# Attention with decay and a feed-forward block: plain float32 scores for eight heads, and another pace for the weights

## The chip, the cores and the metric

The kernel runs on one NeuronCore of a Trainium2 chip. TensorE (PE) multiplies matrices and transposes through an identity, VectorE (DVE), ScalarE (ACT) and GpSimd (POOL) do the elementwise work, and SyncE (SP) issues all DMA transfers of this kernel, in program order. Each engine runs its own instructions in order and waits on semaphores for the others. The metric is the device time of one execution, in microseconds (us).

## The reference

There are 8 batches of 8 heads, 576 tokens, 64 numbers a head. With `q`, `k`, `v` and a forget gate `f`:

```python
scores = scale * np.matmul(q, k.transpose(0, 1, 3, 2))      # scale = 1/8
log_f = np.log(np.clip(f, 0.0001, 1.0))
cum = np.cumsum(log_f, axis=-1)
decay = cum[:, :, :, None] - cum[:, :, None, :]
scores = np.where(causal, -1000000000.0, scores + decay)
scores = scores - np.max(scores, axis=-1, keepdims=True)
attn = np.exp(scores)
attn = attn / (np.sum(attn, axis=-1, keepdims=True) + 1e-09)
out = np.matmul(attn, v)
```

The heads of a batch are put side by side as `x` (4608 tokens of 512), and a block with a hidden layer of 2048 follows:

```python
xn = (x - mean) / np.sqrt(var + 1e-06) * g_ln
return x + np.maximum(xn @ w_ch1, 0.0) @ w_ch2
```

All is float32, except that the two weight matrices come as float64. `q` and `k` are some six times larger than in a usual draw, about 0.6 in spread.

## The kernel before, in words

**Precision.** Two ways of multiplying are used. In one, an operand is split into a high part (type `fp32r`, made by a copy on ScalarE) and the remainder (a subtraction on GpSimd or VectorE), and products of the parts are added up in PSUM. In the other, plain float32 operands go straight into the matmul. The heads 0 to 15 (`h.full`, `NFULL = 16`) use plain float32 for attention times v (`av_unit`, L464); the heads 16 to 63 use split operands there (L486). The scores use split operands in all heads.

**Preparing a head's scores.** `load` (L303) brings `raw`, both q and k transposed, with the 64 rows present twice on the 128 partitions. `prep_a` copies k to its high part (L323) and loads two decay rows into `kl` (L322, for head 0 L119); `prep_b` subtracts for k's remainder on GpSimd (L326) and copies q (L330); `prep_c` moves q's high part by DMA into `xq` (L333) and subtracts for q's remainder on GpSimd (L334). There is one `raw` buffer, and there are two each of `hi`, `kl` and `xq`. `xq` has two rows of ones at its end (L319), which meet the decay rows. A score tile is then two matmuls (L353 of 128 rows, L354 of 66 rows) over the same columns; a head has 64 + 192 + 320 + 448 + 576 = 1600 columns in five tiles.

**Slots.** A head is four slots, t = 1 to 4; slot u = 4n + t - 1. Slot t = 1 computes two query tiles (64 and 128 queries), the others one of 128. In a slot, a string of letters (`ORDERS`) gives the order in which the pieces are issued, the same order on every engine. Until slot 37 it is `WwQsSthAeMrgFBmlLNPaRf`. Q is the score matmuls; S the masked minimum of the negative scores on VectorE (L377); e the exponential on ScalarE (L388); B the reciprocal of the row sum on VectorE (L393, L394) and the scaling on GpSimd (L395). t transposes the tile of two slots ago on PE (L401), h copies the transposes on ScalarE (L451), A is attention times v of three slots ago. P prepares later heads: `prep_a`, `prep_b`, `prep_c` of the next head in t = 1, 2, 3, and the raw load of the head after it in t = 4. M, r, m, N, R are the feed-forward part ("MoE steps").

**Weights.** The float64 weights come as pairs of 32-bit words and are turned to float32 on the chip, in 32 items (16 of each matrix, taking turns). One item is started in each tick of `WPrep.tick`. An item costs one scaling on ScalarE (L162), three integer operations on VectorE (L172, L173, L176), a copy to its high part on ScalarE (L213) and a remainder on GpSimd (L217); items of the first matrix also have eight matmul records for column sums (L188) and four operations on VectorE (L196). The letter W calls ticks until a due count is reached:

```python
due = 1 + min(u, W_CHANGE) / W_SLOTS + max(0, u - W_CHANGE) * W_TICKS
while not wp.done() and wp.tick_no <= due:
    wp.tick()
```

Its operations are put in a queue, from which w, g and f take one, two and three in each slot; a new tick first empties the queue. All ticks together are 38.

**MoE steps.** A chunk is 256 tokens; there are 18 chunks of 16 steps. A step is 12 matmuls into the hidden layer (L563 to L565), a relu and its remainder (L571 on ScalarE, L576 on VectorE), and six matmuls of the step before (L585 to L587). At most one step is made in each slot from slot 35 on (`FIRST_MOE`), if its data are there: step j of a chunk needs 2(j + 1) weight items, where `ready()` counts the ticks less five. Chunks 0 and 1 need batch 0 alone, the next ones later batches. What is left when the slots are over follows in a loop of its own.

Of the kernel before, what the change touches and what calls it, by code (L numbers as in the profile page):

```python
# [8 lines left out]
F32 = mybir.dt.float32  # L9
F32R = mybir.dt.float32r  # L10
# [5 lines left out]
B, H, S, D = 8, 8, 576, 64  # L16
# [7 lines left out]
S1 = 320  # L24
NEG = -1.0e9
SCALE = 1.0 / 8.0
NFULL = 16
W2_LOW = 3
W2_WAIT = 2
# [2 lines left out]
FIRST_MOE = 35  # L32
WARM = 36

W_SLOTS, W_CHANGE, W_TICKS = 1.85, 68, 1.1
W_RAW, W_FLOAT = 3, 5
W_BORROW = 2
W_SUMS = 2
# [19 lines left out]
def attn_moe(ctx: ExitStack, tc: tile.TileContext, qk, v, f, g, w1, w2, out):  # L58
    nc = tc.nc

    const = ctx.enter_context(tc.tile_pool(name="const", bufs=1))
    work = ctx.enter_context(tc.tile_pool(name="work", bufs=1))
# [6 lines left out]
    mm = nc.tensor.matmul  # L69

    def bank(name):
        return ps.tile([P, 512], F32, tag="b", bufs=6, name=name)
# [12 lines left out]
    for i in range(WARM):  # L85
# [4 lines left out]
        out=mask[:, S - P :], in_=mask[:, S - P :], pattern=[[-1, P]], base=0,  # L90
# [9 lines left out]
    cumr = work.tile([B * H, 2, S], F32R, tag="ph2", bufs=1, name="cumr")  # L100
    cumd = dram.tile([B * H, 2, S], F32, tag="cumd", name="cumd")
# [9 lines left out]
    def gates(h0):  # L111
        nc.vector.tensor_scalar(out=fa, in0=fa, scalar1=1e-4, scalar2=1.0, op0=ALU.max, op1=ALU.min)
        nc.scalar.activation(fb, fa, AF.Ln)
        nc.vector.tensor_tensor_scan(out=fc, data0=fones, data1=fb, initial=0.0, op0=ALU.mult, op1=ALU.add)
        nc.scalar.activation(cumr[:, 0, :], fc, AF.Copy, scale=-1.0 / SCALE)
        nc.vector.scalar_tensor_tensor(
            out=cumr[:, 1, :], in0=fc, scalar=-1.0 / SCALE, in1=cumr[:, 0, :].bitcast(F32), op0=ALU.mult, op1=ALU.subtract
        )
        nc.sync.dma_start(out=h0.kl[64:66, :].bitcast(F32), in_=cumr[0:1].bitcast(F32))  # L119
        nc.sync.dma_start(out=cumd, in_=cumr.bitcast(F32))  # L120


# [2 lines left out]
    def consts():  # L125
        nc.sync.dma_start(out=gcol, in_=g)
        nc.gpsimd.memset(gneg, -1.0 / DM)
        nc.gpsimd.tensor_tensor(
            out=gneg.rearrange("p (k c) -> p k c", k=KT), in0=gneg.rearrange("p (k c) -> p k c", k=KT),
            in1=gcol.rearrange("p (k o) -> p k o", o=1).broadcast_to((P, KT, P)), op=ALU.mult,  # L130
        )
# [162 lines left out]
    class Head:  # L294
        pass

    xqs = []

    def load(n):
        h = Head()  # L300
        h.n, h.full = n, n < NFULL
        h.raw = late.tile([P, 2, S], F32, tag="raw", bufs=1, name=f"raw{n}")
        nc.sync.dma_start(out=h.raw, in_=qk[n])  # L303
        return h
# [8 lines left out]
    def prep_a(h):  # L313
        n = h.n
        h.hi = late.tile([P, 2, S], F32R, tag="hi", bufs=2, name=f"hi{n}")
        h.kl = work.tile([66, S], F32R, tag="kl", bufs=2, name=f"kl{n}")
        if len(xqs) < 2:
            xqs.append(work.tile([66, S], F32R, tag="xq", bufs=2, name=f"xq{n}"))
            nc.gpsimd.memset(xqs[n][64:66, :].bitcast(F32), 1.0)  # L319
        h.xq = xqs[n % 2]  # L320
        if n > 0:
            nc.sync.dma_start(out=h.kl[64:66, :].bitcast(F32), in_=cumd[n])  # L322
        nc.scalar.copy(out=h.hi[:, 1, :], in_=h.raw[:, 1, :])  # L323

    def prep_b(h):
        nc.gpsimd.tensor_tensor(  # L326
            out=h.kl[0:64, :], in0=h.raw[0:64, 1, :], in1=h.hi[0:64, 1, :].bitcast(F32), op=ALU.subtract
        )

        nc.scalar.copy(out=h.hi[:, 0, :], in_=h.raw[:, 0, :])  # L330

    def prep_c(h):
        nc.sync.dma_start(out=h.xq[0:64, :].bitcast(F32), in_=h.hi[0:64, 0, :].bitcast(F32))  # L333
        nc.gpsimd.tensor_tensor(  # L334
            out=h.hi[64:128, 0, :], in0=h.raw[64:128, 0, :], in1=h.hi[64:128, 0, :].bitcast(F32), op=ALU.subtract
        )
# [8 lines left out]
    def qk_mm(h, t):  # L345
        q0, m, w = QT[t]
        cuts = [(0, w)] if w <= 512 else [(0, w // 2), (w // 2, w)]
        h.s = getattr(h, "s", {})
        h.s[t] = []
        for i, (a, z) in enumerate(cuts):  # L350
            sp = bank(f"s{h.n}_{t}_{i}")[:m, : z - a]
            xq, kl = h.xq[:, q0 : q0 + m], h.kl[:, a:z]
            mm(sp, h.hi[:, 0, q0 : q0 + m], h.hi[:, 1, a:z], start=True, stop=False)  # L353
            mm(sp, xq, kl, start=False, stop=True)  # L354
            h.s[t].append((a, z, sp))

    corners = []
# [9 lines left out]
    def softmax_a(h, t):  # L367
# [8 lines left out]
        for i, (a, z, sp) in enumerate(h.s[t]):  # L376
            nc.vector.tensor_tensor_reduce(  # L377
                out=pt[:m, a:z], in0=sp, in1=mask[:m, off + a : off + z], scale=-SCALE,
                scalar=3.0e38 if i == 0 else st[:m, 0:1], op0=ALU.add, op1=ALU.min, accum_out=st[:m, i : i + 1],
# [69 lines left out]
    def transposed_hi(h, t):  # L449
        for tp, hi, lo in h.parts:  # L450
            nc.scalar.copy(out=hi, in_=tp)  # L451
# [280 lines left out]
    hd = {}  # L732

    def start_head(n):
        hd[n] = load(n)
# [4 lines left out]
    wp.load(1)  # L740
    load_v(hd[0])
    consts()
    prep_a(hd[0])
    prep_b(hd[0])
    prep_c(hd[0])
    start_head(1)
    gates(hd[0])
    wp.tick()
    for u, slot in enumerate(slots):

        def before(k):
            return slots[u - k] if u >= k else None

        if slot is not None:
            n, t = slot
            h = hd[n]
        av = None
        if before(LAG + 1) is not None and before(LAG + 1)[1] in (2, 4):
            av = hd[before(LAG + 1)[0]]
        moe.fetch_low(ALL if wp.done() else wp.ready())  # L760
        want = moe.can(wp.ready()) and u >= FIRST_MOE

        def piece(c):
            tu = before(LAG)
            if c == "t" and tu is not None:
                transpose_unit(hd[tu[0]], tu[1])
            elif c == "h" and tu is not None:
                transposed_hi(hd[tu[0]], tu[1])
            elif c == "l" and tu is not None:
                transposed_lo(hd[tu[0]])  # L770
            elif c == "Q" and slot is not None:
                if t == 1:
                    qk_mm(h, 0)
                qk_mm(h, t)
            elif c == "A" and av is not None:
                av_unit(av, before(LAG + 1)[1])
            elif c == "S" and slot is not None:
                if t == 1:
                    softmax_a(h, 0)
                softmax_a(h, t)  # L780
            elif c == "e" and slot is not None:
                if t == 1:
                    softmax_e(h, 0)
                softmax_e(h, t)
            elif c in FILL:
                wp.fill(FILL[c])
            elif c == "s":
                wp.sums()
            elif c == "F" and av is not None:
                finish(av)  # L790
            elif c == "a" and av is not None:
                finish_add(av)
            elif c == "r" and want:
                moe.first_high()
            elif c == "R":
                moe.limit = min(NCHUNK, max(0, u - LAG - 1) // (4 * H) * S // C)
                moe.rest()
            elif c == "L":
                run_later(RSTD)
            elif c == "M" and want:  # L800
                moe.first()
            elif c == "B" and slot is not None:
                if t == 1:
                    softmax_b(h, 0)
                softmax_b(h, t)
            elif c == "m" and want:
                moe.first_low()
            elif c == "W":
# [3 lines that stand above are left out]
            elif c == "N":  # L812
                moe.second()
            elif c == "P":
                prep()

        def prep():

            if slot is not None:
                if n + 1 < B * H:  # L820
                    if t == 1:
                        prep_a(hd[n + 1])
                    if t == 2:
                        prep_b(hd[n + 1])
                    if t == 3:
                        prep_c(hd[n + 1])
                if t == 4 and n + 2 < B * H:
                    start_head(n + 2)
                if not h.full and t == LAG + 1:
                    prep_v(h)  # L830
                if t == LAG + 1 and n + 1 < B * H:
                    load_v(hd[n + 1])

        for c in [o for first, o in ORDERS if first <= u][-1]:
            piece(c)
# [48 lines left out]
```

## Time and profile before

| | |
|---|---|
| median of 3 runs | 1301.36 us (1301.26 to 1301.51) |
| profiled execution | 1305.8 us |
| its span, first to last instruction | 1304.0 us |
| PE / DVE / ACT / POOL busy, share of the span | 95% / 61% / 50% / 35% |
| mean granted clock of TensorE | 0.962 |
| DMA moved | 194.33 MB, 149 GB/s |

Busy time counts how long an engine has an instruction in it. For PE the ends of matmuls are modelled, since they are pipelined: the distance between two starts says more than a duration. "PEclk" or "granted clock" is the share of the full clock that TensorE got. A row of an instruction group reads: line, engine, operation, output <- inputs, shape and count, then busy time and mean duration in ns, then the idle time of the engine just before and what ended it. A row of the timeline reads: start, duration, engine, line, operation, and in brackets the idle time before it with its releaser. "SPq" rows are the issue of a DMA by SyncE.

### The profile page before, as it was taken

The page shows a single profiled execution, that of the slowest core. Times are in us where ns is not written, and L with a number is a line of the kernel's source. Part 1 is how long each engine was busy: PE and PEld are TensorE (multiplying, and loading weights), DVE is VectorE, ACT ScalarE, POOL GpSimd, SP SyncE. Part 2 cuts the span into 40 slices and gives each one's busy share as a digit, 9 for nine tenths or more (in the row PEclk, how much of TensorE's full clock was granted, in tenths as well). Part 3 has the DMA queues.
Part 4 walks back from the last instruction along what each step waited for, and adds up shares of the span by engine and source line. Part 5 has one row for each costly group of instructions (what it writes and reads, how often), then busy time and mean ns, then how long its engine had stood idle before and what let it go on. Part 6 is the DMA issues. An engine that isn't in the chain of part 4 may idle for free.

```text
span 1304.0 us, 25602 instructions
## 1 busy us (share of the span) xinstructions
PE 1243.2 (95%) x8148; PEld 1099.5 (84%) x8148; DVE 794.0 (61%) x2868; ACT 657.8 (50%) x1937; POOL 450.5 (35%) x543
## 2 busy tenths in 40 slices
PE   4888698989999999999999999999999999999998
PEld 4565486669999999998999999999999999999997
DVE  4776757756767676767676767676767652232232
ACT  4666556655555555655555555555556531111111
POOL 4556545544343434343334343434343400000000
PEclk7777799999999999999999999999999999999999
DMA  4565466335454545454545454544554434444433
GB/s 151 159 207 174 148 208 178 111 127 162 137 172 135 175 134 175 134 175 134 175 134 175 133 175 134 169 140 156 152 158 151 152 103 141 122 124 127 131 117 94
DMA packets 139895, 194.33 MB, mean 149 GB/s; under 512 B 32496, under 2 KB 81648, under 8 KB 139760
## 3 DMA queue, kind: packets, MB, share of 16 engines
q1 hardware_dynamic: 139760, 192.69, 47.8%
q8 instruction: 65, 1.06, 0.3%
q14 instruction: 70, 0.57, 0.1%
HBM read 159.82 MB, written 23.36 MB: 140 GB/s over the span
## 4 chain that ended last, share of the span: by engine, by line
PE 79%; DVE 6%; DMA 6%; ACT 4%; POOL 2%; issue 2%; SPq 0%; POOLq 0%; ACTq 0%; DVEq 0%
PE h L564 10%; PE h L563 10%; PE acc L585 9%; PE h L565 9%; PE acc L586 9%; PE acc L587 9%; PE tr L401 6%; PE o L486 5%; DMA raw<-in_qk_dram 4%; PE s L353 3%; PE o L464 3%; PE s L354 3%; ACT p L388 1%; POOL hi L334 1%; PE xp L401 1%
## 5 line engine op out<-in xcount | busy, mean ns | idle before, releaser
L395 POOL TENSOR_SCALAR p<-p,st 64x64 f32<-64x64 f32 (+4 forms) x320 | 176.2, 553 | 566.6 <-DVE st L394 266.1
L563 PE MATMUL h<-x,w1h 128*128 128x256 f32 x1152 | 329.9, 286 | 4.4 <-ACT x L547 4.4
L564 PE MATMUL h<-x,w1h 128*128 128x256 f32 x1152 | 327.0, 284 | 1.2 <-DVE x L548 0.6
L565 PE MATMUL h<-x,w1l 128*128 128x256 f32 x1152 | 325.2, 282 | 0.0
L571 ACT ACTIVATE hh<-h 128x256 fp32r<-128x256 f32 x288 | 110.7, 384 | 311.4 <-PE h L565 307.5
L576 DVE SCALAR_TENSOR_TENSOR hh<-h,hh 128x256 fp32r<-128x256 f32 x288 | 121.6, 422 | 212.4 <-ACT hh L571 204.5
L585 PE MATMUL acc<-w2h,hh 128*128 128x512 f32 x576 | 229.2, 398 | 0.6 <-ACT hh L571 0.6
L563 PEld LDWEIGHTS h<-x,w1h 128*128 128x128 f32 x1152 | 218.4, 190 | 10.7 <-ACT x L547 5.4
L586 PE MATMUL acc<-w2s,hh 128*128 128x512 f32 x576 | 227.3, 395 | 0.0
L587 PE MATMUL acc<-w2h,hh 128*128 128x512 f32 x576 | 226.6, 393 | 0.0
L564 PEld LDWEIGHTS h<-x,w1h 128*128 128x128 f32 x1152 | 218.7, 190 | 6.6 <-DVE x L548 3.0
L565 PEld LDWEIGHTS h<-x,w1l 128*128 128x128 f32 x1152 | 218.5, 190 | 0.0
L388 ACT ACTIVATE p<-p,st 64x64 f32<-64x64 f32 (+4 forms) x320 | 178.4, 559 | 62.2 <-DVE st L377 59.1
L451 ACT CAST ph<-tr 64x128 fp32r<-64x128 f32 (+4 forms) x384 | 108.9, 333 | 119.3 <-PE tr L401 88.9
L353 PE MATMUL s<-hi 128*128 128x288 f32 (+4 forms) x384 | 132.7, 366 | 37.8 <-POOL hi L334 35.4
L401 PE MATMUL tr<-identr,p 128*128 128x128 f32 (+1 forms) x896 | 147.4, 283 | 4.0 <-POOL p L395 3.2
L377 DVE CUSTOM_DVE_ANT_0 p<-s,mask 64x64 f32<-64x64 f32 (+4 forms) x320 | 130.6, 420 | 14.6 <-PE s L354 13.1
L587 PEld LDWEIGHTS acc<-w2h,hh 128*128 128x128 f32 x576 | 108.7, 189 | 25.6 <-DVE st L393 0.2
L401 PEld LDWEIGHTS tr<-identr,p 128*128 128x128 f32 (+1 forms) x896 | 105.5, 135 | 24.7 <-POOL p L395 5.4
L456 DVE TENSOR_TENSOR ph<-tr,ph 64x192 fp32r<-64x192 f32 x192 | 57.8, 301 | 106.5 <-ACT ph L451 104.1
L585 PEld LDWEIGHTS acc<-w2h,hh 128*128 128x128 f32 x576 | 109.3, 190 | 14.2 <-issue 0.8
L586 PEld LDWEIGHTS acc<-w2s,hh 128*128 128x128 f32 x576 | 109.5, 190 | 12.4
(79 smaller groups left out, 1900.3 us busy)
## 6 DMA issues: line engine op xcount, KB each, us to landing
w2s<-w2d SPq DMA_DIRECT2D x288, 256.0 KB
raw<-in_qk_dram SPq DMA_DIRECT2D x64, 576.0 KB
wr<-in_w_dram SPq DMA_DIRECT2D x32, 512.0 KB
vr<-in_v_dram SPq DMA_DIRECT2D x64, 160.0 KB
xq<-hi SPq DMA_DIRECT2D x64, 144.0 KB
out_dram<-xt SPq DMA_DIRECT2D x36, 256.0 KB
xa<-xs SPq DMA_DIRECT2D x32, 160.0 KB
w2d<-wl SPq DMA_DIRECT2D x16, 256.0 KB
```

Source lines behind the costliest of these rows:

```text
L353: mm(sp, h.hi[:, 0, q0 : q0 + m], h.hi[:, 1, a:z], start=True, stop=False)
L377: nc.vector.tensor_tensor_reduce(out=pt[:m, a:z], in0=sp, in1=mask[:m, off + a : off + z], scale=-SCALE, scalar=3.0e38 if i == 0 else st[: ...
L388: nc.scalar.activation(pt[:m, :w], pt[:m, :w], AF.Exp, bias=st[:m, i : i + 1], scale=-1.0, accum_out=st[:m, 2:3])
L395: nc.gpsimd.tensor_scalar(out=pt[:m, :w], in0=pt[:m, :w], scalar1=st[:m, 3:4], scalar2=1.0, op0=ALU.mult, op1=ALU.mult)
L401: nc.tensor.transpose(out_, in_, ident[:m, :m])
L563: mm(ph, w1h[:, k, fs], c.x[k][:, 0, :], start=(k == 0), stop=False)
L564: mm(ph, w1h[:, k, fs], c.x[k][:, 1, :], start=False, stop=False)
L565: mm(ph, w1l[:, k, fs], c.x[k][:, 0, :], start=False, stop=(k == KT - 1))
L576: nc.vector.scalar_tensor_tensor(out=h[:, 1, :], in0=ph, scalar=0.0, in1=h[:, 0, :].bitcast(F32), op0=ALU.max, op1=ALU.subtract)
L585: mm(c.acc[i], h[:, 0, ts_], w2h[:, j, :], start=(j == 0), stop=False)
L586: mm(c.acc[i], h[:, 0, ts_], low, start=False, stop=False)
L587: mm(c.acc[i], h[:, 1, ts_], w2h[:, j, :], start=False, stop=(j == FT - 1))
```

## The change

For the heads 0 to 7 (`NPLAIN = 8`) q and k are loaded straight into `xq` and `kl` as float32, 64 rows each, together with the decay rows, by three DMAs issued in slot t = 1 of the head before. There is no `raw`, no high part and no remainder for these heads, and a score tile is one plain float32 matmul of 66 rows in place of two. The heads from 8 on are prepared as before. At the start, the preparation of head 0 and the load of head 1's `raw` ahead of the gate computation go away. The weights' due count is changed to 1 + u / 2.4 until slot 34, and from there on 0.95 ticks are added in each slot; before, it was 1 + u / 1.85 until slot 68.

```diff
+NPLAIN = 8
...
-W_SLOTS, W_CHANGE, W_TICKS = 1.85, 68, 1.1
+W_SLOTS, W_CHANGE, W_TICKS = 2.4, 34, 0.95
...
-    xqs = []
+    xqs, xfs = [], []
+
+    def new_xq(name, dt):
+        xq = work.tile([66, S], dt, tag="xq", bufs=2, name=name)
+        nc.gpsimd.memset(xq[64:66, :].bitcast(F32), 1.0)
+        return xq
 
     def load(n):
         h = Head()
-        h.n, h.full = n, n < NFULL
+        h.n, h.plain, h.full = n, n < NPLAIN, n < NFULL
+        if h.plain:
+            h.kl = work.tile([66, S], F32, tag="kl", bufs=2, name=f"kl{n}")
+            if len(xfs) < 2:
+                xfs.append(new_xq(f"xf{n}", F32))
+            h.xq = xfs[n % 2]
+            nc.sync.dma_start(out=h.xq[0:64, :], in_=qk[n][0:64, 0, :])
+            nc.sync.dma_start(out=h.kl[0:64, :], in_=qk[n][0:64, 1, :])
+            if n > 0:
+                nc.sync.dma_start(out=h.kl[64:66, :], in_=cumd[n])
+            return h
...
-            mm(sp, h.hi[:, 0, q0 : q0 + m], h.hi[:, 1, a:z], start=True, stop=False)
-            mm(sp, xq, kl, start=False, stop=True)
+            if h.plain:
+                mm(sp, xq, kl, start=True, stop=True)
+            else:
+                mm(sp, h.hi[:, 0, q0 : q0 + m], h.hi[:, 1, a:z], start=True, stop=False)
+                mm(sp, xq, kl, start=False, stop=True)
...
     consts()
-    prep_a(hd[0])
-    prep_b(hd[0])
-    prep_c(hd[0])
-    start_head(1)
     gates(hd[0])
...
-                if n + 1 < B * H:
+                if t == 1 and n + 1 < NPLAIN:
+                    start_head(n + 1)
+                if NPLAIN <= n + 1 < B * H:
                     if t == 1:
                         prep_a(hd[n + 1])
...
-                if t == 4 and n + 2 < B * H:
+                if t == 4 and NPLAIN <= n + 2 < B * H:
                     start_head(n + 2)
```

More of the change, by code (lines that the diff above doesn't have):

```diff
@@ L118, in gates @@
         )
-        nc.sync.dma_start(out=h0.kl[64:66, :].bitcast(F32), in_=cumr[0:1].bitcast(F32))
+        nc.sync.dma_start(out=h0.kl[64:66, :], in_=cumr[0:1].bitcast(F32))
         nc.sync.dma_start(out=cumd, in_=cumr.bitcast(F32))
@@ L317, in prep_a @@
         if len(xqs) < 2:
[L318 to L322, printed above, removed]
+            xqs.append(new_xq(f"xq{n}", F32R))
+        h.xq = xqs[(n - NPLAIN) % 2]
+        nc.sync.dma_start(out=h.kl[64:66, :].bitcast(F32), in_=cumd[n])
         nc.scalar.copy(out=h.hi[:, 1, :], in_=h.raw[:, 1, :])
```

## The prediction

> **What bounds the kernel now.** I read the clock by slices first, then the span cut at the starts of heads 0, 1, 8 and 18, then the waits of the first stretch, then single instructions.
>
> ```profile
> PEclk7777799999999999999999999999999999999999
> ```
> ```profile
> 134.55 0.31 PE L353 MATMUL s<-hi 128*64 128x64 f32 x1 [3.61 <-POOL hi L334]
> ...
> 300.19 0.28 PE L353 MATMUL s<-hi 128*64 128x64 f32 x1
> ```
> ```profile
> 0.00:19.40 19.40, 7.24 (x38) 6.87 (x38) 7.58 (x8) 7.58 (x9) 7.50 (x15) 0.79 0.47 149
> 19.40:31.60 12.20, 6.01 (x26) 5.22 (x26) 7.80 (x28) 6.63 (x19) 5.23 (x7) 0.64 0.54 164
> 31.60:134.60 103.00, 83.26 (x358) 57.75 (x358) 73.72 (x230) 66.23 (x191) 62.23 (x64) 0.73 0.56 173
> 134.60:300.20 165.60, 148.07 (x846) 114.27 (x846) 109.61 (x360) 98.25 (x291) 84.96 (x91) 0.92 0.52 160
> 300.20:1304.00 1003.80, 998.65 (x6887) 915.40 (x6884) 595.24 (x2244) 479.12 (x1430) 290.63 (x367) 1.00 0.47 145
> ```
> The columns are the stretch, its length, busy time of PE, PEld, DVE, ACT and POOL, the granted clock, DMA share and GB/s. The 64-query score matmul opens each head, so the two rows above date heads 8 and 18. From 300.2 us on PE is busy for 998.65 of 1003.80 us at full clock: whatever matmul work is left there sets the end, and each MoE step done earlier comes straight off it. The loss lies ahead: at 134.6 us no MoE step has run, and PE was idle for a fifth of the time and slow for much of the rest.
>
> ```profile
> PE s L353 <- POOL hi L334: 24.4, 8, 4.7
> ...
> DVE st L393 <- ACT p L388: 21.2, 17, 2.4
> ...
> DVE p L377 <- PE s L354: 7.9, 9, 3.1
> ```
> These are waits from 20 to 134.6 us (total us, times, longest). Nearly all of PE's idle time, 24.4 us, is the first score matmul of a head waiting for GpSimd's remainder of q (L334), which the change drops for heads 0 to 7. VectorE's own idle time is mostly the wait for the exponentials, 21.2 us, which stays.
>
> **The start (term A).**
> ```profile
> 3.59 0.45 DVE L112 TENSOR_SCALAR fa<-fa 64x576 f32<-64x576 f32 x1 [1.68 <-DMA fa<-in_f_dram]
> ...
> 5.97 0.67 ACT L323 CAST hi<-raw 128x576 fp32r<-128x576 f32 x1 [3.96 <-DMA raw<-in_qk_dram]
> ...
> 8.53 0.68 ACT L113 ACTIVATE fb<-fa 64x576 f32<-64x576 f32 x1
> 9.32 1.35 DVE L114 TENSOR_TENSOR_SCAN fc<-fones,fb 64x576 f32<-64x576 f32 x1 [5.28 <-ACT fb L113]
> ...
> 11.42 0.99 DVE L116 SCALAR_TENSOR_TENSOR cumr<-fc,cumr 64x576 fp32r<-64x576 f32 x1 [0.75 <-ACT cumr L115]
> ...
> 16.28 0.73 SPq L119 DMA_DIRECT2D kl<-cumr  x1
> ...
> 19.38 0.18 PEld L354 LDWEIGHTS s<-kl,xq 66*64 66x64 f32 x1 [3.33 <-DMA kl<-cumr]
> ```
> Head 0 really starts at 19.4 us, when its two decay rows have landed. Those rows were ready at 12.4, but their issue stood on SP behind head 1's raw load, which waited for L334; and the logarithm started at 8.53 though its input was ready at 4.04, because ScalarE held two casts that waited for the raw load until 5.97. Without both, and with the logarithm's table loaded while its input is under way: Ln at 4.1, scan at 4.8, then the same steps as from 9.32 to 12.41 (3.1 us) to 7.9, issue, and landing 3.1 us after it (16.28 to 19.38): 11.0. Gain 8.4 us. q and k, second and third on SP and together half of the raw load, must land by then; the whole of that load was there at 5.97, which is ample.
>
> **Heads 0 to 7 (term B).** Plain scores cost PE more, and the fences give the price.
> ```profile
> 75.11 0.24 PE L353 MATMUL s<-hi 128*64 128x64 f32 x1 [1.97 <-POOL hi L334]
> ...
> 76.18 2.80 PE L464 MATMUL o<-ph,vr 64*64 64x320 f32 x6
> 78.91 0.64 PE L353 MATMUL s<-hi 128*128 128x320 f32 x1
> ...
> 83.39 2.30 PE L464 MATMUL o<-ph,vr 64*64 64x256 f32 x10
> 85.62 0.40 PE L353 MATMUL s<-hi 128*128 128x288 f32 x1
> ...
> 88.74 0.24 PE L353 MATMUL s<-hi 128*64 128x64 f32 x1 [1.97 <-POOL hi L334]
> ```
> ```profile
> 75.11:88.74 13.63, 11.65 (x52) 8.06 (x52) 9.77 (x33) 9.44 (x27) 8.70 (x9) 0.75 0.63 182
> 76.20:82.90 6.70, 6.70 (x24) 4.90 (x24) 5.26 (x16) 4.08 (x12) 3.69 (x5) 0.51 0.64 180
> 82.90:88.70 5.80, 3.86 (x22) 2.33 (x19) 3.42 (x13) 5.35 (x16) 3.95 (x4) 1.00 0.56 153
> ```
> This is head 4. Float32 A·V streams 704 columns in 2.73 us at half clock (3.9 ns a column) and 1152 in 2.23 us at full clock (1.9 ns). A head's scores are 1600 columns: 3.1 us at full clock, 6.2 at half, about 4.2 in this mixture, against the 2.7 or so that the pairs take now. I charge 1.5 us a head. The Trainium skill (FP8 and Floating Point Precision, TensorE Precision Notes) says that true FP32 takes four passes through the array, which speaks against the change: two passes become four. By that rule the charge would be a doubling, 2.7 us a head or 10 us more over eight heads; the A·V rows are that four-pass product at work, so I keep their price.
>
> On PE's side a head now takes 11.65 us busy and 2 idle. With the idle time gone and 1.5 added it is 13.1, if the half-clock stretch of 6.7 us stays. That stretch follows the idle gap; without it it shrinks by up to 3.4 us, to 9.7.
>
> ```profile
> L173 DVE SCALAR_TENSOR_TENSOR wy<-wy,wr 128x512 uint32<-128x512 uint32 x17 | 21.3, 1255 | 0.0
> ...
> L176 DVE SCALAR_TENSOR_TENSOR wy<-wr,wy 128x512 uint32<-128x512 uint32 x17 | 16.8, 991 | 0.3
> ...
> L326 POOL TENSOR_TENSOR kl<-raw,hi 64x576 fp32r<-64x576 f32 x8 | 11.2, 1404 | 0.0
> L334 POOL TENSOR_TENSOR hi<-raw,hi 64x576 fp32r<-64x576 f32 x8 | 11.2, 1401 | 0.7
> L196 DVE SCALAR_TENSOR_TENSOR wy<-wy,gcol,pc 128x128 f32<-128x128 f32 x32 | 10.7, 337 | 0.0
> L172 DVE TENSOR_SCALAR wr<-wr 128x512 uint32<-128x512 uint32 x16 | 7.8, 488 | 1.7 <-ACT wy L162 1.7
> ```
> Then VectorE is next to be late. A tick costs it 1.26 + 0.99 + 0.49 + two of 0.34 = 3.4 us. By slot 31 the old rule has called for 18 ticks, 1 + 31/1.85, and the new one for 14, 1 + 31/2.4: 12 us less (allowing for overlap of records). The 22.4 us that leave GpSimd, and two casts a head that leave ScalarE, shorten its waits. From the three stretch rows, heads 0 to 7 take 115.2 us, with VectorE busy about 81.5; less 12 and 2 for fewer collisions with GpSimd is 67.5, and with some 28 us of waits for exponentials and other engines it is 95.5, or 11.9 a head. PE's two values lie around that. I take 12.2, so 97.6 us: a gain of 17.6. Bounds are 13.6 a head (gain 6) and 10.9 (gain 28).
>
> The new loads are issued in slot 1 of the head before, three slots or 9 us ahead of use; they cost nothing under that cover. They wait on SP for the score matmuls two heads back, done a slot earlier, and weight loads queue behind; if that cover failed, each head would lose about the 3.1 us of a landing. The two memsets of ones move from head preparation to the loads and cost GpSimd the same. Head 8 is prepared as before, so its first matmul still waits. A and B: **-26 us**.
>
> **Slots 32 to 71 (terms C and D).**
> ```profile
> L563 PE MATMUL h<-x,w1h 128*128 128x256 f32 x76 | 23.4, 308 | 3.6 <-ACT x L547 3.6
> ```
> ```profile
> 160.00:239.70 79.70, 75.63 (x445) 59.38 (x445) 54.26 (x160) 47.42 (x136) 38.66 (x39) 0.94 0.57 175
> 239.70:300.20 60.50, 52.76 (x320) 40.99 (x317) 37.92 (x153) 35.46 (x109) 31.60 (x37) 0.97 0.45 139
> ```
> ```profile
> 1201.45 0.28 PE L563 MATMUL h<-x,w1h 128*128 128x256 f32 x1
> ...
> 1204.26 0.28 PE L563 MATMUL h<-x,w1h 128*128 128x256 f32 x1
> ```
> 76 such matmuls between 134.6 and 300.2 us are 19 MoE steps of four. A step is 2.81 us of PE at full clock. Step j of the first chunk needs 2(j+1) weight items, so the 16 steps of chunk 0 end when the counter shows 37: about slot 65 now, slot 56 with 0.95 ticks a slot. From then on every slot can hold a step, so at head 18 about 30 steps are done instead of 19: 11 x 2.81 = **-31 us** (D) after it.
>
> They have to be paid for ahead of it (C). In the first stretch (160 to 239.7, slots 38 to 55) ticks rise by some 8, at 3.0 to 3.6 us of VectorE: 54.3 + 24 to 29 is 78 to 83 of 79.7 us, so VectorE is full, and waits of 7 or so make about 88. PE has three steps more and four column sums: 75.6 + 8.4 + 4 = 88. I take 91: +11. In the second stretch eight steps are 22.5 us of PE, of which its 7.7 idle us take some: +15, bounds +12 and +24. Heads 8 and 9 lose nothing. C is **+26**, between +14 (VectorE hidden) and +45 (each tick at twice its rise).
>
> **Sum.** 1304.0 - 26 + 26 - 31 = 1273. The profiled execution lasted 1305.8 around its span, the median of the runs is 1301.4, 2.6 below the span: **1270 us**.
>
> **Rivals.** (1) PE stays half slow in heads 0 to 7: other gaps of 2 us arise and B is 6. Each row of the slow stretch speaks for it; against it, VectorE-paced idle time comes in small pieces. 1304 - 14 - 5 - 2.6 = 1282.
> (2) The clock stays full from head 0 and VectorE hides its ticks: B 28, C +14, thus 1304 - 36 - 17 - 2.6 = 1248. For it: nothing makes PE wait 2 us any more. Against it: at 75.11 an idle gap of 1.97 us was enough to halve the clock. The Trainium skill (TensorE: Matmul & The Clock Gate, HAM oscillation) puts the limit at gaps over about 3.4 us; by that rule this rival would be the rule, and this trace does not agree.
> (3) VectorE binds in slots 38 to 55 with PE waiting a little each slot: C +40, so 1284.
> (4) Slower: the same place, but every collision is long, as in the last of the three figures (shortest, median, longest) of these rows.
> ```profile
> L173 DVE SCALAR_TENSOR_TENSOR wy<-wy,wr x32: 676/1310/1866, 12.8 to 244.2; 128x512 uint32<-128x512 uint32 x32
> ```
> ```profile
> L176 DVE SCALAR_TENSOR_TENSOR wy<-wr,wy x32: 678/972/1806, 14.6 to 245.1; 128x512 uint32<-128x512 uint32 x32
> ```
>  If a tick costs VectorE 1.87 + 1.81 + 0.49 + 0.67 = 4.8 us and its exponentials are uncovered as well, heads 9 to 13 take 29 us each instead of 18, C +60 or more, and PE starves at half clock. It decides from C = 57 on, where A, B and D are used up; at +65 the time is 1309. Against it: the mean rows are well below that, and VectorE is now only 68% busy there.
>
> **Chances.** Forecast, 1260 to 1278: 0.48. Rival 1: 0.16, rival 2: 0.14, rival 3: 0.13, rival 4: 0.09. The range of 8 in 10 reaches from rival 2 past rival 3: 1249 to 1292. A measurement of this kernel can tell 0.2%, 2.6 us, from no change. Rival 4 is slower in most of its cases, 0.08; within the bound lie 0.04, from its mild end and the far end of rival 3; faster is 0.88.
>
> **What would show it.** Right: no score matmul waiting for GpSimd in heads 0 to 7; first score matmul near 11 us; head 8 near 108; head 18 near 300 with 30 steps behind it; VectorE above 90% between heads 9 and 13. Wrong: a clock still near 0.73 in heads 0 to 7 (rival 1), heads 9 to 13 above 24 us each (rivals 3 and 4), or PE no longer full behind head 18.

## The result, and the profile after

The changed kernel takes 1254.98 us in the median, against 1301.43 us before: a ratio of 0.9659, with a 95% interval of 0.9623 to 0.9695. Measured once more in a later series it gave 1254.54 us and 0.9646 (0.9630 to 0.9661). Its runs lie further apart than those of the kernel before, from 1252.2 to 1262.7 us, and the first profiled run (span 1260.6 us) is the longest of them. I therefore show a second profiled run of the same kernel beside it (span 1252.0 us). All medians and ratios here are of runs in the usual state; one of the four runs of the pace alone, at a mean clock of 0.739, took 1510.34 us and is left out.

The first profile's page, with the clock in 40 slices:

```profile
span 1260.6 us, 25515 instructions
...
PEclk7799899999999999999999999999999999999999
```

The stretches of the first profile, cut at the starts of heads 0, 8 and 18 (columns as in the prediction), and the matmul group that counts the MoE steps between head 8 and head 18:

```profile
0.00:9.90 9.90, 6.57 (x37) 6.36 (x37) 5.47 (x8) 4.79 (x6) 3.96 (x12) 1.00 0.52 168
9.90:107.50 97.60, 88.35 (x367) 54.33 (x367) 63.93 (x240) 60.98 (x189) 42.83 (x56) 0.83 0.52 152
107.50:288.10 180.60, 167.75 (x1050) 136.46 (x1050) 126.44 (x392) 107.01 (x311) 90.49 (x95) 0.97 0.58 181
288.10:1260.60 972.50, 967.56 (x6698) 888.03 (x6696) 586.98 (x2232) 472.39 (x1416) 289.48 (x367) 1.00 0.47 146
```
```profile
L580 PE MATMUL h<-x,w1h 128*128 128x256 f32 x116 | 35.1, 303 | 0.0
```

The same cuts in the second profile of the changed kernel:

```profile
9.90:96.70 86.80, 77.25 (x367) 47.47 (x367) 63.24 (x237) 60.28 (x187) 42.85 (x56) 0.94 0.60 171
96.70:279.20 182.50, 171.64 (x1048) 139.67 (x1049) 126.47 (x392) 107.49 (x313) 90.98 (x95) 0.95 0.58 178
279.20:1252.00 972.80, 967.41 (x6699) 888.05 (x6697) 588.12 (x2232) 473.89 (x1417) 289.38 (x367) 1.00 0.47 146
```

Head 0 starts at 9.9 instead of 19.4 us. Heads 0 to 7 take 97.6 us in one profile and 86.8 in the other, instead of 115.2. Heads 8 to 17 take 180.6 and 182.5 instead of 165.6, but 116 matmuls of four a step are 29 MoE steps, where there were 19. What lies behind head 18 shrinks from 1003.8 to 972.5 and 972.8. So the first profile is 9.5 + 17.6 - 15.0 + 31.3 = 43.4 us shorter than that of before, the second 9.5 + 28.4 - 16.9 + 31.0 = 52.0.

The two profiles are of the same program and differ in heads 1 to 3, where the clock differs. The same 30 us of each, the first profile and then the second:

```profile
14.00:44.00 30.00, 29.97 (x88) 18.79 (x89) 14.74 (x56) 14.44 (x44) 8.17 (x13) 0.50 0.41 108
```
```profile
14.00:44.00 30.00, 28.31 (x137) 18.23 (x137) 21.36 (x82) 21.09 (x67) 12.16 (x18) 0.93 0.63 169
```

In the first, TensorE was busy without a break by the profile and stood at half clock all the time: 88 matmul records in the time in which the second did 137. The size fits: a mean clock of 0.83 over 97.6 us is 16.6 us of full clock lost, 0.94 over 86.8 us is 5.2 us, and the difference of 11.4 us is close to the 10.8 us between the two.

### The profile page after: what moved, and what is told of

It reads as the page before. It is cut to its first block, busy times and chain, and to the rows that moved or that the text cites. A ratio compares the mean times of both kernels' runs of the same rounds, so it can differ in the third digit from the quotient of the medians.

```text
span 1260.6 us, 25515 instructions
## 1 busy us (share of the span) xinstructions
PE 1230.2 (98%) x8148; PEld 1085.2 (86%) x8148; DVE 782.8 (62%) x2868; ACT 645.2 (51%) x1920; POOL 426.8 (34%) x529
## 4 chain that ended last, share of the span: by engine, by line
PE 86%; DVE 5%; DMA 4%; ACT 1%; POOL 1%; issue 1%; SPq 0%; DVEq 0%; POOLq 0%; ACTq 0%
PE h L580 11%; PE h L581 10%; PE h L582 10%; PE acc L602 10%; PE acc L603 10%; PE acc L604 10%; PE tr L418 7%; PE o L503 5%; PE o L481 3%; PE s L370 3%; PE s L371 3%; DMA raw<-in_qk_dram 3%; PE s L368 1%; PE xp L418 1%; DVE wy L174 1%
## 5 line engine op out<-in xcount | busy, mean ns | idle before, releaser
L418 PE MATMUL tr<-identr,p 128*128 128x128 f32 (+1 forms) x896 | 143.7, 277 | 9.0 <-POOL p L412 4.7
L394 DVE CUSTOM_DVE_ANT_0 p<-s,mask 64x64 f32<-64x64 f32 (+4 forms) x320 | 130.3, 420 | 15.5 <-PE s L368 9.8
L418 PEld LDWEIGHTS tr<-identr,p 128*128 128x128 f32 (+1 forms) x896 | 102.9, 132 | 35.3 <-POOL p L412 9.1
L370 PE MATMUL s<-hi 128*64 128x64 f32 x336 | 109.8, 349 | 8.3 <-POOL hi L348 6.5
```

The costliest lines, as they stand in the source:

```text
L394: nc.vector.tensor_tensor_reduce(out=pt[:m, a:z], in0=sp, in1=mask[:m, off + a : off + z], scale=-SCALE, scalar=3.0e38 if i == 0 else st[: ...
L418: nc.tensor.transpose(out_, in_, ident[:m, :m])
```

## The experiments

### One half of the change at a time

Plain scores with the weights' old pace:

```diff
-W_SLOTS, W_CHANGE, W_TICKS = 2.4, 34, 0.95
+W_SLOTS, W_CHANGE, W_TICKS = 1.85, 68, 1.1
```

> Plain scores for heads 0 to 7, with the weights' old pace (1.85 slots a tick to slot 68). Theory S (the terms of the prediction stand for themselves): the start and the missing wait for GpSimd stay, four ticks more fall into heads 0 to 7, and MoE steps come no earlier, so head 8 starts near 117 us, heads 8 to 17 take their old 166 us, and the time is near 1284 us. Rival R (the pace makes nearly all of the gain, since PE was only waiting for what VectorE would have delayed anyway): 1293 us or more.

The new pace alone, in the kernel before:

```diff
-W_SLOTS, W_CHANGE, W_TICKS = 1.85, 68, 1.1
+W_SLOTS, W_CHANGE, W_TICKS = 2.4, 34, 0.95
```

> The new pace of the weights alone, with split scores everywhere. Theory S: heads 0 to 7 still wait for GpSimd's remainder, head 8 starts 0 to 6 us earlier than before, and heads 8 to 17 gain the 13 us that they show in the changed kernel (15 us longer, ten steps of 2.81 us more): 1283 to 1288 us. Rival R: 1265 us or less. Should both parts alone add up to far less than the 46 us, they need each other.

Plain scores alone: 1272.5 us, ratio 0.9767 (0.9736 to 0.9799). The pace alone: 0.9844 (0.9815 to 0.9873), 1280.7 us. The stretches of plain scores alone, cut at heads 0, 8 and 18 (this profile is of the fastest of its four runs, 1268.2 us):

```profile
9.90:103.40 93.50, 82.79 (x384) 51.13 (x384) 76.03 (x257) 65.18 (x196) 48.61 (x60) 0.91 0.62 187
103.40:262.90 159.50, 143.16 (x846) 111.68 (x846) 108.87 (x360) 97.62 (x291) 85.51 (x92) 0.95 0.54 166
262.90:1266.40 1003.50, 998.78 (x6887) 915.28 (x6884) 595.77 (x2244) 478.94 (x1430) 289.55 (x367) 1.00 0.47 145
```

And of the pace alone, from the landing of the decay rows on:

```profile
19.00:125.40 106.40, 86.26 (x367) 58.10 (x367) 69.81 (x236) 68.01 (x200) 61.02 (x67) 0.71 0.53 161
125.40:306.50 181.10, 171.33 (x1049) 139.12 (x1050) 126.71 (x392) 108.02 (x313) 90.12 (x94) 0.95 0.58 179
306.50:1278.20 971.70, 966.90 (x6699) 887.95 (x6697) 587.16 (x2232) 473.64 (x1417) 289.44 (x367) 1.00 0.47 146
```

The gains of the two halves add up to 3.9% where the whole gives 3.4 to 3.5%, so the halves do not need each other, and rival R falls on both counts. Plain scores gain 12 us more than theory S gave them: with 18 ticks in heads 0 to 7 as before, these heads take 93.5 us, not the 106 or so that 117 us for head 8 meant. The pace alone is near where theory S put it, 2 us or so below its 1283 to 1288: heads 8 to 17 get 15.5 us longer and the rest 32 shorter, as it said, but head 8 starts 9.2 us earlier than before (125.4 against 134.6), not 0 to 6.

### The early and the late half of the pace

```diff
-W_SLOTS, W_CHANGE, W_TICKS = 2.4, 34, 0.95
+W_SLOTS, W_CHANGE, W_TICKS = 1.85, 34, 0.95
```

> The old pace up to slot 34 (1.85 slots a tick), then the new 0.95 ticks a slot. It splits the pace into its halves. If the slow start is what pays, as term B has it, heads 0 to 7 lose 7 to 10 us again and the time is 1262 us or more. If only the fast end pays, the four ticks moved back leave slots 35 to 57, where VectorE is full, and the time stays within 3 us of the changed kernel.

1253.21 us, 0.9633 (0.9619 to 0.9646), beside 0.9646 (0.9630 to 0.9661) for the changed kernel in the same series. Its stretches, and its step count between the same two heads:

```profile
9.90:103.20 93.30, 82.58 (x383) 51.20 (x383) 76.34 (x257) 64.89 (x195) 48.36 (x60) 0.90 0.63 187
103.20:291.80 188.60, 183.36 (x1104) 149.04 (x1105) 117.24 (x395) 106.07 (x311) 85.33 (x91) 0.94 0.54 166
```
```profile
L580 PE MATMUL h<-x,w1h 128*128 128x256 f32 x132 | 40.5, 307 | 0.2 <-DVE st L410 0.2
```

Both branches of the expectation hold in part: heads 0 to 7 lose 6.5 us against the second profile, and the time stays. But most of the loss is the clock of this one run. Its 0.90 over 93.3 us is 9.3 us of full clock lost, 4 more than in the second profile, and head 1 alone takes 15.7 us instead of 9.5, at a mean clock of 0.59 against 1.00. Heads 2 to 7 had the same clock in both, here and then in the second profile:

```profile
33.60:103.20 69.60, 61.67 (x307) 38.27 (x306) 60.47 (x201) 52.46 (x157) 40.58 (x46) 0.97 0.65 197
```
```profile
28.70:96.70 68.00, 60.63 (x299) 37.05 (x298) 50.57 (x187) 49.08 (x151) 36.66 (x44) 0.97 0.58 171
```

VectorE is busy for 9.9 us more there, and the heads take 1.6 us more. The four ticks done early also let the steps come earlier still, 33 instead of 29 by head 18. Slowing the weights down at the start is worth nothing that these runs can measure; the late half of the pace is worth the step from 0.9767 to 0.9633, 17 us.

### The start alone

Only head 0 has plain scores (`NPLAIN = 1`), the pace is the old one, and head 1's raw load is issued before the gates as it was.

> Only head 0 has plain scores, and the weights keep their old pace, so of the prediction's terms only A, the earlier start, is left. If the start comes straight off the end: 9 us less than the kernel before, 1292 to 1294 us. Rival: heads 1 to 8 go by their own chains and the 9 us are given back at the first wait for GpSimd: 1298 us or more.

1294.21 us, 0.9946 (0.9930 to 0.9961): 7 us. Head 1 starts at 22.0 us instead of 31.6, and still waits for GpSimd:

```profile
22.04 0.32 PE L370 MATMUL s<-hi 128*64 128x64 f32 x1 [4.46 <-POOL hi L348]
```

Term A goes nearly straight to the end. Some 2 us of the earlier start seem to be lost on the way, but the interval, 5.1 to 9.1 us, leaves that open.

### Is it the wait, or the work behind it?

The changed kernel, with the old preparation of heads 2 to 7 put back as work that nobody reads: the raw load, two casts and two subtractions a head. The DMA that moves q's high part is not put back.

```diff
+    def dead_load(n):
...
+        nc.sync.dma_start(out=d.raw, in_=qk[n])
...
+    def dead_prep(n, t):
+        d = dead[n]
+        if t == 1:
+            d.hi = late.tile([P, 2, S], F32R, tag="hi", bufs=2, name=f"dhi{n}")
+            nc.scalar.copy(out=d.hi[:, 1, :], in_=d.raw[:, 1, :])
+        if t == 2:
+            nc.gpsimd.tensor_tensor(
+                out=d.hi[0:64, 1, :], in0=d.raw[0:64, 1, :], in1=d.hi[0:64, 1, :].bitcast(F32), op=ALU.subtract
+            )
+            nc.scalar.copy(out=d.hi[:, 0, :], in_=d.raw[:, 0, :])
+        if t == 3:
+            nc.gpsimd.tensor_tensor(
+                out=d.hi[64:128, 0, :], in0=d.raw[64:128, 0, :], in1=d.hi[64:128, 0, :].bitcast(F32), op=ALU.subtract
+            )
...
+                if n + 1 < NPLAIN and t < 4:
+                    if n > 0:
+                        dead_prep(n + 1, t)
+                if t == 4 and 1 < n + 2 < NPLAIN:
+                    dead_load(n + 2)
```

> The changed kernel, in which heads 2 to 7 have their old preparation as work that nobody reads: the raw load, two casts on ScalarE and two subtractions on GpSimd a head, at their old places. PE waits for none of it. Theory W (what the change takes off GpSimd and ScalarE is worth something of its own, by fewer collisions and a free ScalarE): heads 0 to 7 take 5 us more or over, 1259 us or more. Rival O (only PE's wait for the remainder counted): within 3 us of the changed kernel, 1252 to 1257 us.

1270.6 us, 0.9756 (0.9735 to 0.9777): 14 us more than the changed kernel in the series before it. Rival O falls. Theory W has the right side; of its two reasons, the free ScalarE is seen in the trace and the collisions are small. Heads 0 to 7 of this kernel, three rows from its timeline (with that kernel's own line numbers: L353 is the added cast), and its two longest stretches at half clock:

```profile
9.90:117.00 107.10, 96.96 (x368) 58.61 (x368) 66.88 (x238) 66.84 (x200) 61.40 (x68) 0.75 0.57 172
```
```profile
67.56 0.67 ACT L353 CAST dhi<-draw 128x576 fp32r<-128x576 f32 x1 [2.12 <-DMA draw<-in_qk_dram]
...
68.66 0.63 ACT L493 COPY ph<-tr 64x128 f32<-64x128 f32 x2
...
68.97 3.23 PE L506 MATMUL o<-ph,vr 64*64 64x256 f32 x10 [1.99 <-ACT ph L493]
```
```profile
36.10:60.00 23.90, 23.60 (x64) 13.67 (x64) 12.38 (x39) 13.31 (x40) 14.17 (x14) 0.50 0.42 125
70.20:87.30 17.10, 17.10 (x50) 10.21 (x49) 10.12 (x35) 10.50 (x32) 10.72 (x11) 0.50 0.51 147
```

VectorE is busy for 66.9 us, 3.6 more than the 63.2 of the second profile, so collisions with it are a small part. PE is busy for 97.0 instead of 77.3 us with 368 records instead of 367, at a mean clock of 0.75 instead of 0.94. ScalarE stops 2.1 us for a raw load, its copy of the transposes comes late behind that, and PE waits 2.0 us for the copy; 1.2 us later the clock falls, for 17.1 us. The stretch from 36.1 us stands behind two shorter waits of PE, 1.23 us for GpSimd and 0.30 us for ScalarE; a wait of 0.86 us stands at the same place in the second profile, without a fall. The price fits the clock: 0.75 over 107.1 us is 26.8 us of full clock lost, 21.6 more than in the second profile, and heads 0 to 7 are 20.3 us longer. Nor is it one run: the mean clock of these four runs is 0.973 to 0.983, against 0.985 to 0.989 for the changed kernel in its second series. So the work is dear mainly by the time that PE spends at half clock while it is there. That the holes in PE's stream bring the clock down is read from their order in time, not shown by a run of its own, and not every hole does: one of 1.51 us at 99.4 us of the first profile was followed by full clock.

### The clock

Two measures against the half-clock stretch. Rows of zeros fill q and k up to 128 rows:

```diff
-        xq = work.tile([66, S], dt, tag="xq", bufs=2, name=name)
+        xq = work.tile([P if dt == F32 else 66, S], dt, tag="xq", bufs=2, name=name)
+        if dt == F32:
+            nc.gpsimd.memset(xq[64:128, :], 0.0)
...
-            h.kl = work.tile([66, S], F32, tag="kl", bufs=2, name=f"kl{n}")
+            h.kl = work.tile([P, S], F32, tag="kl", bufs=2, name=f"kl{n}")
+            nc.gpsimd.memset(h.kl[64:128, :], 0.0)
```

> The changed kernel with q and k of heads 0 to 7 filled up with rows of zeros, so that the plain score matmul has 128 rows instead of 66; results and streamed columns are the same. It asks why TensorE stood at half clock from 14 to 44 us although it had no idle time there. Theory F (the clock follows how much of the array the matmuls fill): the half-clock stretch shrinks to about 7 us, and the time falls to about 1245 us. Rival G (the clock falls by the idle gaps of 1.4 to 1.7 us between 8.5 and 13.6 us, and the rows do not matter): the stretch stays, 1253 to 1262 us.

Idle transposes of the identity fill PE's gaps at the start:

```diff
-WARM = 36
+WARM = 44
...
+            if c == "Q" and u < 2:
+                if u == 0:
+                    warm2 = ps.tile([P, DM], F32, tag="acc0", bufs=1, name="warm2")
+                for i in range(10):
+                    nc.tensor.transpose(warm2[:, 0:P], ident, ident)
```

> The changed kernel with idle transposes of the identity that fill the gaps of TensorE at the start: 44 instead of 36 ahead of head 0, and ten behind the score matmuls of slots 0 and 1. Theory G: the clock never falls in heads 0 to 2, which then take about 10 to 12 us instead of 13 to 17, and the time is 1240 to 1248 us. Theory F: the clock falls as soon as head 0's own matmuls are alone, and the time stays at 1253 to 1262 us.

Then both together, and the changed kernel as it is, in one series:

> Both measures for the clock in one: 128 rows in the plain score matmul, and idle transposes in the gaps at the start. If they act on the same stretch (14 to 44 us), the time is that of either alone, 1249 to 1253 us; if each takes away half-clock time of its own, about 1244 us and a mean clock of 0.995.

> The changed kernel again, beside the two that keep the clock up, on one chip. If the time at half clock is chance, its mean clock lies anywhere between 0.981 and 0.993 here; if it belongs to the kernel, all its runs stay at 0.987 or below and near 1255 us.

| | median us | ratio (95%) | mean clock of its runs |
|---|---|---|---|
| changed kernel, first series | 1254.98 | 0.9659 (0.9623 to 0.9695) | 0.981 to 0.987 |
| changed kernel, again | 1254.54 | 0.9646 (0.9630 to 0.9661) | 0.985 to 0.989 |
| 128 rows | 1252.9 | 0.9627 (0.9598 to 0.9656) | 0.989 to 0.994 |
| idle transposes | 1250.26 | 0.9607 (0.9579 to 0.9636) | 0.984 to 0.993 |
| both | 1250.16 | 0.9610 (0.9596 to 0.9624) | 0.992 to 0.994 |

With both, the kernel is faster than the changed kernel of the same series, with intervals that do not overlap: some 4.7 us. With either alone the interval still touches that of the changed kernel. Together they do no more than the transposes alone, so they seem to act on the same stretch. From 14 to 44 us, where the two profiles of the changed kernel had 0.50 and 0.93, the kernel with 128 rows and then the one with both show:

```profile
14.00:44.00 30.00, 28.63 (x142) 18.49 (x143) 22.12 (x84) 21.48 (x68) 15.43 (x23) 0.94 0.60 165
```
```profile
14.00:44.00 30.00, 27.98 (x143) 17.13 (x142) 22.25 (x83) 21.59 (x68) 15.51 (x23) 1.00 0.60 170
```

A step of the mean clock from 0.986 to 0.993 over 1250 us is 2 x 0.007 x 1250 = 17 us less at half clock, an estimate from the mean.

Neither theory is settled. The second profile of the changed kernel left half clock at 18 us with 66 rows and without added transposes, so how long the stretch lasts varies from run to run. With the zero rows alone no run lies below the highest clock of the changed kernel, 0.989, which speaks for F; that waits of 1.4 and 1.6 us stand before the fall in the first profile speaks for G; and both can be true. Nor are the transposes a sure cure: one of their four runs has a mean clock of 0.984, and with twelve plain heads (below) the clock fell in spite of them. Shown is that both measures together raise the clock of the runs, and that this is worth some 4.7 us.

### VectorE in slots 38 to 55

The changed kernel without the third integer operation of each weight item; it leaves out the lowest three bits of the weights.

```diff
-                lambda: ve.scalar_tensor_tensor(
-                    out=y, in0=low, scalar=29, in1=y, op0=ALU.logical_shift_right, op1=ALU.bitwise_or
-                ),
```

> The changed kernel without the third integer operation of each weight item, which puts in the lowest three bits of the weights: some 1 us less of VectorE in each tick, about 18 us of it between heads 8 and 13. Theory V (VectorE is what slots 38 to 55 wait for): heads 9 to 13 take some 10 us less and the time is 1240 to 1246 us. Rival P (PE with its steps is the bound there already): 3 us less at most.

1246.42 us, 0.9587 (0.9564 to 0.9609): 7.7 us less than the changed kernel of its series, between the two expectations. Heads 9 to 13 in the second profile of the changed kernel, then here:

```profile
111.60:208.50 96.90, 89.84 (x533) 71.94 (x534) 81.74 (x223) 60.67 (x170) 56.33 (x55) 0.93 0.65 202
```
```profile
105.10:198.30 93.20, 88.58 (x533) 70.45 (x534) 66.91 (x210) 60.92 (x169) 57.40 (x55) 0.90 0.64 208
```

VectorE loses 15 us there and the stretch only 3.7. Heads 9, 10 and 11 keep their 20.3 to 20.7 us each, and PE, with a step in every slot, is busy there for 58.2 of 61.2 us in the second profile, so it is PE that holds them. Heads 12 and 13 get shorter, 16.8 and 14.6 us instead of 18.3 and 17.5 (18.6 and 15.9 in the first profile). Another 4.5 us come from heads 0 to 7. VectorE binds in patches, not through the whole stretch.

### More plain heads

With the idle transposes, ten heads instead of eight (`NPLAIN = 10`), and twelve:

> Plain scores for ten heads instead of eight, with the idle transposes at the start. In the changed kernel heads 8 and 9 still wait for GpSimd, 6.5 us together, and the clock falls behind these waits. If this is what is left to gain, 1242 to 1246 us; if heads 8 and 9 wait for VectorE instead as soon as the remainder is gone, 1248 to 1252 us, as with eight heads.

> The same with twelve heads. Heads 10 and 11 have an MoE step in each slot, so PE is the bound there and pays some 1.5 us more for each plain head: slower than ten heads by 2 to 3 us. If instead the preparation is what holds these heads, faster than ten by as much.

Ten heads: 1244.54 us, 0.9571 (0.9547 to 0.9594), against 0.9607 (0.9579 to 0.9636) for eight with the same transposes: better in the median, with intervals that overlap. Twelve: 1250.92 us, 0.9614 (0.9591 to 0.9637), in the median some 6 us slower than ten, twice the expected loss, with intervals that just overlap. Heads 0 to 8 and heads 9 to 11 of the kernel with ten plain heads, then of the one with twelve:

```profile
9.90:103.10 93.20, 86.42 (x447) 54.28 (x447) 72.67 (x266) 66.03 (x207) 45.45 (x61) 1.00 0.63 176
103.10:165.80 62.70, 58.14 (x346) 46.00 (x345) 54.60 (x143) 41.01 (x113) 37.10 (x36) 0.95 0.68 210
```
```profile
9.90:109.10 99.20, 92.08 (x447) 57.23 (x447) 72.76 (x266) 66.77 (x207) 45.38 (x61) 0.93 0.58 166
109.10:172.30 63.20, 59.65 (x346) 45.67 (x345) 51.34 (x143) 38.90 (x109) 29.97 (x30) 0.97 0.65 198
```

With ten, nine heads take 93.2 us at full clock from end to end. With twelve, the same nine heads, with the same 447 matmul records, take 99.2 us at 0.93: of the 6.3 us between these two profiles 6.0 lie there, where the two kernels do the same work but for one raw load at the end. Heads 9 to 11 differ by 0.5 us: heads 10 and 11 take 21.8 and 21.7 us with plain scores instead of 20.4 each, close to the 1.5 us expected, and head 9, whose next head no longer needs its preparation, takes 19.7 instead of 21.9. So the loss is in these profiles the clock at the start, and the other runs go the same way: the mean clock is 0.996 in four of five runs with ten plain heads, and 0.986 to 0.996 with twelve. What two plain heads with a step in every slot cost net is 0.5 us here. Ten plain heads with the transposes have the best median of all versions here, and are faster than both kernels: the interval ends below that of the changed kernel.

## Why the prediction was right, and where its sizes were off

1270 us were forecast, 1255 measured: the direction, the range (1249 to 1292) and the order of the terms hold, and the gain came out half as large again as forecast.

**Where the end is set.** Right. Behind head 18 PE is busy for 967.56 of 972.50 us, and moving steps ahead of it paid in full. D was put at 31 us, and that part is 31.3 us shorter, but with 10 steps (28 us) instead of 11; eight transposes for a later chunk also moved ahead, and the rest of the 3 us is not accounted for. That the figure agrees so closely is luck. Head 18 starts at 288 and 279 us, not near 300, with 29 steps done.

**A, the start.** 11.0 us forecast, 9.9 measured. The chain is the one described: the logarithm at 4.27, the issue of the decay rows at 7.94.

```profile
4.27 0.68 ACT L114 ACTIVATE fb<-fa 64x576 f32<-64x576 f32 x1 [2.24 <-DVE fa L113]
...
7.94 0.73 SPq L120 DMA_DIRECT2D kl<-cumr  x1
...
9.88 2.11 PE L368 MATMUL s<-kl,xf 66*64 66x64 f32 x8 [1.36 <-DMA kl<-cumr]
```

The landing took 1.9 us in place of 3.1. Of the gain, 7 us reach the end when head 0 stands alone.

**The price of plain scores.** Right for a column. The rows are the first profile's, 320 columns at half clock and 576 at full clock, each with the instruction behind it:

```profile
23.79 1.44 PE L368 MATMUL s<-kl,xf 66*128 66x320 f32 x2
...
25.02 1.06 PE L418 MATMUL tr<-identr,p 128*64 128x128 f32 x4
```
```profile
47.83 1.24 PE L368 MATMUL s<-kl,xf 66*128 66x288 f32 x4
48.90 0.49 PE L418 MATMUL tr<-identr,p 128*64 128x128 f32 x3
```

1.23 us for 320 is 3.8 ns a column, 1.07 us for 576 is 1.9: the prices taken from A·V, to the tenth. The prediction set a doubling of the price against this, and the doubling came too. A pair of 288 columns at full clock in the kernel before, and the instruction behind it:

```profile
86.00 0.30 PE L353 MATMUL s<-hi 128*128 128x288 f32 x1
...
86.27 0.49 PE L401 MATMUL tr<-identr,p 128*64 128x128 f32 x3
```

That is 0.27 us, where a plain tile of 288 columns takes 0.53. For 1600 columns the difference is 1.5 us, an estimate from these two, and it is the charge that the prediction made. The two prices were one; the 2.7 us a head that it would have doubled were pairs run in part at half clock.

**B, heads 0 to 7.** B and C are the terms that were mis-sized. The sum gave a span of 1273; the first profile is 12.4 us below it, of which C is 11.0, and the second 21.0 us, of which B is 10.8 and C 9.1. For B, 12.2 us a head were forecast. The first profile has 97.6 us for the eight, to the tenth the forecast sum, but by chance: 14 to 44 us of it ran at half clock, which is rival 1, and heads 4 to 6 took 9.7 to 11.6 us, which is rival 2. The second profile, nearer to the median run, has 10.9 a head, the lower bound. The step that failed is "Then VectorE is next to be late", with the heads' time made up of 67.5 us busy and 28 of waits. In the second profile it is 63.2 busy and 23.6 idle; with the old early pace, 76.3 busy and 17.0 idle. The waits are not a fixed sum on top of VectorE's work: in heads 2 to 7, at the same clock, 9.9 us more of it cost 1.6. So VectorE's total is not what sets the time of these heads, though its operations are not free: without the low bits the eight heads take 4.5 us less. What moved them most from one run to the next is the clock.

The busy time itself is below the forecast because two operations of a tick got shorter, in the first profile (1.26 and 0.99 us before) and then in the run with the dead preparation:

```profile
L174 DVE SCALAR_TENSOR_TENSOR wy<-wy,wr 128x512 uint32<-128x512 uint32 x13 | 12.4, 951 | 0.0
L177 DVE SCALAR_TENSOR_TENSOR wy<-wr,wy 128x512 uint32<-128x512 uint32 x13 | 11.5, 886 | 0.2
```
```profile
L174 DVE SCALAR_TENSOR_TENSOR wy<-wy,wr 128x512 uint32<-128x512 uint32 x13 | 12.3, 946 | 0.0
L177 DVE SCALAR_TENSOR_TENSOR wy<-wr,wy 128x512 uint32<-128x512 uint32 x14 | 14.4, 1030 | 0.3
```

The second operation is longer again when GpSimd's subtractions are back. The first is not, so collisions with these subtractions do not explain its fall, and why it fell stays open.

The 12 us credited to fewer ticks were therefore not a gain of the change: with the old early pace heads 2 to 7 lose 1.6 us and the end does not move. What the prediction credited in B it charged again in C, so the sum was spared. "No score matmul waits for GpSimd in heads 0 to 7" holds; head 8 still does:

```profile
107.50 0.24 PE L370 MATMUL s<-hi 128*64 128x64 f32 x1 [2.83 <-POOL hi L348]
```

**C, slots 32 to 71.** +26 forecast, +15 and +17 measured. Heads 9 to 13 and 14 to 17 of the first profile:

```profile
121.40:217.30 95.90, 87.49 (x533) 70.03 (x534) 82.14 (x223) 60.71 (x170) 56.31 (x55) 0.95 0.65 204
217.30:288.10 70.80, 70.80 (x460) 59.59 (x458) 33.51 (x138) 37.45 (x116) 24.77 (x31) 1.00 0.48 146
```

They were 89.1 and 60.5 us in the kernel before, so +6.8 and +10.3 against +11 and +15, and head 8 gave 2.2 back. VectorE is at 86%, not above 90% as forecast: the step "so VectorE is full" was too strong, as the run without one of its operations shows. In heads 9 to 11 it is PE, whose 88 us the prediction had beside it. Rivals 3 and 4 fall with it.

**The clock.** Weighed as rivals 1 and 2, and rightly not decided. What the prediction missed is that one kernel would do both, run by run, and that a stretch at half clock can go on for 30 us while PE is busy.

## What to carry to other kernels

When one engine is full to the end, ask of each change how much of that engine's work it moves ahead of the full part; what is gained in front and given back in front cancels, and can be left out of the sum. A slower product that saves preparation on other engines pays as long as the matrix engine has room; where it is full, here from the first head with a step in every slot on, it shows no gain. Do not add an engine's waits to its work as if they were fixed: more work may go into the waits. And the time at half clock can outweigh what a change does, so compare the granted clock of two profiles, stretch by stretch, before putting their difference down to the change.

## What the hardware showed beyond expectation

TensorE can be busy without a break, by the profile, and stay at half clock: 29.97 of 30.0 us at 0.50 in the first profile of the changed kernel. In the kernel before, the half-clock stretch of head 4 was over after 6.7 us, and so was the one at the start of the changed kernel's second profile:

```profile
11.60:18.40 6.80, 5.35 (x19) 3.84 (x18) 3.25 (x15) 2.90 (x11) 1.81 (x4) 0.50 1.07 276
```

So one program can have either. Zero rows and added transposes both came with a higher mean clock; which property of the stream decides is open.

A recorded clock between half and full need not be a slower one. The profile of the run without the low bits has 0.95 behind head 18:

```profile
269.50:1243.00 973.50, 968.47 (x6699) 889.78 (x6696) 587.12 (x2232) 473.85 (x1416) 289.32 (x367) 0.95 0.47 146
```

The second profile of the changed kernel did the same 6699 matmul records in 972.8 us at 1.00. So the pace tells more than the recorded figure, and the clocks of 0.90 and 0.95 in that run's rows are not to be compared with those of the others.
